# A chain of attention and two MoE blocks: seven instead of eight value products per group in the last two and a half batches of MoE2, over one token buffer

## The chip, the cores and the metric

The kernel runs on one core of one Trainium2 chip. The metric is device time in microseconds: the median of three runs of the whole program.

## The reference, cut to what matters

Attention with a bias from relative positions gives `x` (4 batches x 576 tokens, 512 features). MoE1 takes the maximum of three products and multiplies by `w_out`. MoE2, where the change is made, is

```python
gate = 1.0 / (1.0 + np.exp(-(x @ w_gate)))      # x: 2304 x 512, w_gate: 512 x 1536
val = x @ w_val                                 # w_val: 512 x 1536
return (gate * val @ w_out).astype(np.float32)  # w_out: 1536 x 512
```

All products must be exact to float32. The kernel writes each operand as the sum of two float16 halves, a high one and a low one, and adds three products of halves (high x high, high x low, low x high).

## The kernel before, in words

Every instruction is recorded first (class `Recorder`) and then put in order by a list scheduler (`emit`, `choose`): each engine takes from four classes, `BIAS`, `ATT`, `MOE`, `PREP` in falling priority, the instruction that can start first by the planner's own costs. After that the order on each engine is fixed, and an instruction that waits holds up those behind it on its engine.

MoE2 goes over 4 batches (`b`) of 576 tokens and, in each, over 6 groups of weight columns (`i`). One such step is `quad(b, i)`: 256 gate columns and 256 value columns for 576 tokens, as 2 x 2 blocks of 128 columns by 288 tokens over a depth of 2 x 256.

- The gate blocks are made by Strassen's scheme (Winograd's form): 7 products of block sums instead of 8. Each product is a `group` of 6 matmuls (2 depth steps x 3 products of halves) with 288 moving columns into one PSUM bank. VectorE adds the 7 results up in `sg` (L1279 to L1287); ScalarE copies the first (L592).
- The value blocks are made directly: 8 groups of 6 matmuls into two pairs of banks (`two_r`). ScalarE makes the sigmoid (L1298), VectorE multiplies by the value straight from PSUM (L1300), and the product is split into halves (L1306, and L1096 through `add2`).
- So a quad has 90 matmuls on L1269. The gate parts go through two banks (`part_r`), in the order 1, 6, 7, 5, 2, 3, 4.

The moving operands are the block sums of the tokens, `XC`: 8 slots (slot 7 only for the direct value products), each in two halves. `token_sums` loads a batch from `x_d`, makes the sums (`add2`, L1096) and splits each into halves (`halves`: ScalarE L1102, VectorE L1103). There are two buffers `XC_`, used in turn, so a batch's sums are made while the batch before is multiplied: `next_tokens` is called at the start and in the middle of a batch, in class `ATT`.

The stationary operands are `SW[i]`: 7 gate sums and 4 raw value blocks for each `i`, made early in the stage by `pair_weights`, with the decode from float64 words on VectorE (L554 to L556). `out_weights` does the same for `w_out`, into `OW`; its last part must be done before the first product of `outs`.

`outs` multiplies a finished batch by `w_out`: 36 matmuls with 512 columns (L1325), four evacuations on ScalarE (L1333), one store. In batches 1 to 3 one such call stands behind each of the first four quads; five more are at the end of the kernel. For TensorE they are work that can stand in while MoE2's next quad is not ready. Here `BIAS` is the class of all evacuations.

Of the kernel before, what the change touches and what calls it, by code (L numbers as in the profile page):

```python
# [11 lines left out]
F16 = mybir.dt.float16  # L12
# [3 lines left out]
ALU = mybir.AluOpType  # L16
# [97 lines left out]
class Item:  # L114

    __slots__ = ("k", "cls", "alts", "deps", "left", "users", "end", "done", "banks")

    def __init__(self, k, cls):
        self.k, self.cls = k, cls
        self.alts = {}  # L120
        self.deps, self.users = set(), []
        self.left, self.end, self.done = 0, None, False
        self.banks = set()


class Recorder:
# [10 lines left out]
    def __init__(self, nc, untracked):  # L137
        self.nc = nc
        self.untracked = untracked
        self.items, self.first = [], 0  # L140
        self.mem = Mem()
        self.cls = 0
        self.joined = None
        self.t_eng = {e: 0.0 for e in self.WINDOW}
        self.busy = {e: 0.0 for e in self.WINDOW}
        self.t_dma = 0.0
        self.bank = {i: {} for i in range(8)}
        self.lanes = [0.0] * 8
        self.log = []
        self.passed = {e: False for e in self.WINDOW}  # L150
        for attr, eng in self.ENGINES.items():
            setattr(self, attr, Engine(self, getattr(nc, attr), eng))

    def add(self, eng, method, args, kwargs, call):
# [115 lines left out]
    def choose(self, e, lists, force=False):  # L270
# [3 lines left out]
        for c in range(self.NCLS):  # L274
            ks = lists[e][c]
            seen, w = None, 0
            for it in ks:
# [5 lines left out]
                if it.left:  # L283
                    continue
                s = self.start(it, e, self.SPARE[e], self.LATE)
                if len(it.alts) > 1 and not force:
# [167 lines left out]
def tile_kernel(ctx, tc, q, k, v, w1, b1, w2, mw1, mw2, mw3, mwo, gw, vw, ow, xtab, masks, out):  # L454
# [724 lines left out]

    ob_m = X2[:, 3968:4992]  # L1180
# [55 lines left out]

# [15 lines left out]

    part_r, two_r = Ring([bank(i)[:, 0:HS] for i in (5, 6)]), Ring([bank(i, 1024).rearrange("p (a s) -> p a s", a=2)[:, :, 0:HS] for i in (0, 2)])
    RAW = ((0, 1), (7, 2))

    def quad(b, i):

        h0 = 64 * (b % 2)
        ugm = ug[:, b, i:i + 1]
        sg, XC = sg_r(), XC_[b % 2]  # L1260
        c21, c22, c11, c12 = (sg[:, HS * n:HS * (n + 1)] for n in range(4))
# [3 lines left out]
        def group(ps, W, o, x, start, stop):  # L1265
            with nc.join():
                for kk in range(2):
                    for z, (wp, xp) in enumerate(((0, 0), (0, 1), (1, 0))):
                        nc.tensor.matmul(ps, lhsT=W[:, o, wp, kk], rhs=XC[:, x, xp, kk], start=start and kk == z == 0, stop=stop and kk == 1 and z == 2)  # L1269

        vs = []
        for t, n in enumerate((1, 6, 7, 5, 2, 3, 4)):
            ps = part_r()
            group(ps, SW[i][0], WS[n - 1], n - 1, True, True)
            with nc.at(BIAS):
# [12 lines left out]
            if t in (0, 2, 3, 5):  # L1288
                m, hf = ((1, 0), (1, 1), (0, 0), (0, 1))[(0, 2, 3, 5).index(t)]
                if not hf:  # L1290
                    pv = two_r()
                    vs.append((m, pv))
                for kh in range(2):
                    group(pv[:, hf], SW[i][1], 2 * m + kh, RAW[hf][kh], kh == 0, kh == 1)
        with nc.at(BIAS):
            for m, pv in vs:
                at = sg[:, S * m:S * m + S]
                nc.scalar.activation(at, at, AF.Sigmoid, scale=ugm)  # L1298
                at = at.rearrange("p (a s) -> p a s", a=2)
                nc.vector.scalar_tensor_tensor(at, pv, DOWN2, at, op0=ALU.mult, op1=ALU.mult)  # L1300
        g2 = sg.rearrange("p (m s) -> p m s", m=2)
# [39 lines left out]
    for _ in early:  # L1341
        pass
    token_sums(0, Am[:, 18688:19840], Am[:, 19840:20992], Am[:, 20992:21568])
    mems = parts(Am[:, 18688:22784], [1024, 1024, 512, 512, 512, 512]), parts(X2[:, 2816:6912], [1024, 1024, 512, 512, 512, 512])
# [23 lines left out]
    ends = {0: [], 1: [4], 2: [], 3: [4, 5, 6, 7, 8]}  # L1368
    tx = [X2[:, 4992:5568], X2[:, 5568:6144]]

    def next_tokens(b):
        with nc.at(ATT):
            gx = gm_f[(1, 0, 1)[b]]
            token_sums(b + 1, gx[:, 0:1152], gx[:, 3072:4224], tx[b % 2])

    next_tokens(0)
    for b in range(B):
        with nc.at(BIAS):
            batch_scale(b)
            out_scales(b)  # L1380
        for i in range(NP2):
            quad(b, i)
            for ct in after[b].get(i, ()):
                outs((b if b % 2 else b - 1) // 2, ct)
            if i == 3 and 0 < b < B - 1:
                next_tokens(b)
        if b == 1:
# [36 lines left out]
```

## Time and profile before

| | |
|---|---|
| median of 3 runs | 1040.45 us (1037.43 to 1043.86) |
| the profiled execution | 1040.86 us |
| its span, first to last instruction | 1039.1 us |
[...]

MoE2's quads run from 623.97 us to 995.7 us of the span, with outs between them from 715.2 us on; batch 1 begins at 691.8 us. In a profile, PE is TensorE, PEld its weight loads, DVE VectorE, ACT ScalarE. A busy time is a union: instructions that overlap on an engine count once. A duration is that of one instruction, from its start to the end of its write, so that two that follow each other can overlap; the time from one start to the next is shorter.

### The profile page before, as it was taken

How to read it: one execution, taken by the hardware profiler on the slowest of the kernel's cores; microseconds unless marked ns; L12 is line 12 of the kernel's file. 1: busy time of each engine (PE TensorE's matmuls, PEld its weight loads, DVE VectorE, ACT ScalarE, POOL GpSimd, SP SyncE). 2: the span in 40 equal slices, each digit the busy share in tenths (PEclk: the TensorE clock that was granted, in tenths of full speed). 3: DMA queues.
4: the chain of work that ended last, by engine and by line, in shares of the span. 5: the costliest groups of instructions: out<-in, count | busy, mean ns of one | idle time of the engine just before them, and what ended most of it. 6: DMA issues, size and time to landing. Idle time of an engine off the chain costs nothing.

```text
span 1039.1 us, 21298 instructions
## 1 busy us (share of the span) xinstructions
PE 993.7 (96%) x8156; PEld 670.1 (64%) x8156; DVE 722.9 (70%) x1869; ACT 597.6 (58%) x1336; POOL 120.0 (12%) x146
## 2 busy tenths in 40 slices
PE   4898999997999999999999999999999999999998
PEld 2344577664666666677677777876666656766653
DVE  5788998976878789958779989996354335532320
ACT  6898986775787777856765565653233124222221
POOL 1022114342112322112100100000000000000000
PEclk9999999998999999999999999999999999999999
DMA  7896767567999999875686233420010001000001
GB/s 222 252 303 226 271 211 174 164 165 143 213 228 261 234 219 250 206 199 128 146 181 188 82 104 116 138 62 11 11 67 11 11 11 66 2 11 22 11 11 41
DMA packets 172242, 139.49 MB, mean 134 GB/s; under 512 B 111852, under 2 KB 151020, under 8 KB 171628
## 3 DMA queue, kind: packets, MB, share of 16 engines
q1 hardware_dynamic: 169476, 128.39, 47.6%
q10 hardware_dynamic: 2664, 9.74, 3.3%
q8 instruction: 64, 1.05, 0.4%
q14 instruction: 38, 0.31, 0.1%
HBM read 94.25 MB, written 21.23 MB: 111 GB/s over the span
## 4 chain that ended last, share of the span: by engine, by line
PE 77%; DVE 9%; DMA 3%; issue 2%; ACT 2%; POOL 2%; SPq 0%; ACTq 0%; POOLq 0%; DVEq 0%
PE ps L1269 22%; PE ps L945 19%; PE ps L1325 13%; PE ps L890 7%; PE ps L831 5%; PE ps L863 5%; DMA am<-am 2%; PE ps L834 2%; PE ps L669 2%; POOL am L858 1%; DVE am L1103 1%; DVE am L847 1%; DVE wm L975 1%; PE ps L566 1%; PE ps L611 1%
## 5 line engine op out<-in xcount | busy, mean ns | idle before, releaser
L945 PE MATMUL ps<-wm 128*128 128x320 f16 (+2 forms) x2304 | 304.9, 286 | 0.2 <-DVE am L975 0.2
L945 PEld LDWEIGHTS <-wm 128*128 128x128 f16 x2304 | 222.9, 99 | 54.9 <-issue 3.2
L1269 PE MATMUL ps<-am 128*128 128x288 f16 x1800 | 223.9, 286 | 1.3 <-DVE wm L1300 0.7
L1269 PEld LDWEIGHTS <-am 128*128 128x128 f16 x1800 | 176.1, 98 | 48.5 <-issue 1.6
L1325 PE MATMUL ps<-wm 128*128 128x512 f16 x648 | 142.5, 379 | 0.0
L848 ACT ACTIVATE am<-am,small 128x576 f32<-128x576 f32 (+1 forms) x160 | 123.1, 770 | 30.3 <-DVE small L847 19.4
L847 DVE CUSTOM_DVE_ANT_0 am<-ps,am 128x576 f32<-128x576 f32 (+1 forms) x160 | 117.9, 749 | 28.2 <-issue 13.0
L1325 PEld LDWEIGHTS <-wm 128*128 128x128 f16 x648 | 63.3, 98 | 73.5
L858 POOL TENSOR_SCALAR am<-am,small 128x576 f32<-128x576 f32 (+1 forms) x65 | 64.5, 997 | 206.1 <-DVE small L850 135.5
L890 PE MATMUL ps<-am 128*64 128x128 f32 (+4 forms) x980 | 81.0, 313 | 1.1 <-DVE wm L896 0.7
L592 ACT ACTIVATE am<-ps 128x512 f32<-128x512 f32 (+3 forms) x146 | 66.1, 472 | 26.9 <-PE ps L863 23.5
L863 PE MATMUL ps<-ident,am 128*128 128x128 f32 x450 | 72.2, 282 | 7.5 <-POOL am L858 6.1
L863 PEld LDWEIGHTS ps<-ident,am 128*128 128x128 f32 x450 | 51.1, 143 | 26.1 <-POOL am L858 10.4
L1298 ACT ACTIVATE x<-x,ug 128x576 f32<-128x576 f32 x24 | 18.6, 775 | 77.8 <-DVE x L1287 77.7
L831 PE MATMUL ps<-am 64*128 64x512 f16 (+1 forms) x390 | 55.1, 384 | 7.3 <-DMA am<-am 6.8
L1333 ACT ACTIVATE x<-ps,uo 128x128 f32<-128x128 f32 x64 | 18.2, 368 | 75.3 <-PE ps L1325 55.4
L1298 ACT ACTIVATE wm<-wm,ug 128x576 f32<-128x576 f32 x24 | 18.5, 771 | 56.8 <-DVE wm L1287 56.8
L890 PEld LDWEIGHTS ps<-am 128*64 128x64 f32 x680 | 39.5, 137 | 17.8 <-issue 4.9
L872 DVE SCALAR_TENSOR_TENSOR am<-am,small 128x576 f16<-128x576 f32 (+1 forms) x60 | 48.0, 825 | 3.9 <-ACT am L871 3.8
L975 DVE SCALAR_TENSOR_TENSOR wm<-ps,small,wm 128x256 f32<-128x256 f32 (+1 forms) x84 | 43.0, 512 | 8.5 <-PE ps L945 6.8
L1269 PE MATMUL ps<-am,x 128*128 128x288 f16 x360 | 46.0, 286 | 2.5 <-DVE am L1103 1.9
L871 ACT ACTIVATE am<-am,small 128x576 f16<-128x576 f32 (+1 forms) x60 | 43.6, 766 | 5.3 <-ACT am L848 2.7
(180 smaller groups left out, 1382.6 us busy)
## 6 DMA issues: line engine op xcount, KB each, us to landing
am<-bias_d SPq DMA_DIRECT2D x49, 576.0 KB, 4.6
bias_d<-am SPq DMA_DIRECT2D x36, 320.0 KB, 4.4
wm<-in_moe_w_dram SPq DMA_DIRECT2D x12, 768.0 KB, 6.2
am<-bias_d ACTq DMA_DIRECT2D x15, 576.0 KB, 4.9
wm<-in_moe_w_out_dram SPq DMA_DIRECT2D x24, 256.0 KB, 2.9
x<-in_moe_w_val_dram SPq DMA_DIRECT2D x20, 256.0 KB, 4.1
x_d<-wm SPq DMA_DIRECT2D x4, 1152.0 KB, 4.7
am<-in_v_dram SPq DMA_DIRECT2D x16, 256.0 KB, 5.7
```

Of the source, the lines that this page charges most:

```text
L592: nc.scalar.activation(dst, src, AF.Copy, scale=scale)
L831: nc.tensor.matmul(s_main[o][:m], lhsT=q_[h, eq], rhs=k_[h, ek, 0:512], start=(i == 0), stop=(i == 2), tile_position=(64 * o, 0))
L847: nc.vector.tensor_tensor_reduce(e[:m, c], S_[o][:m], bt[:m, c], -1.0, 3.0e38, ALU.add, ALU.min, mx[:m])
L848: nc.scalar.activation(e[:m, c], e[:m, c], AF.Exp, scale=-1.0, bias=mx[:m], accum_out=l[:m, o:o + 1])
L858: nc.gpsimd.tensor_scalar(e[:m, c], e[:m, c], r[:m, o:o + 1], 1.0, op0=ALU.mult, op1=ALU.mult)
L863: nc.tensor.transpose(ps[:, t], e[:, 128 * (t0 + t):128 * (t0 + t) + 128], ident)
L872: nc.vector.scalar_tensor_tensor(ph[:m, 1, c], e[:m, c], f, ph[:m, 0, c], op0=ALU.mult, op1=ALU.subtract)
L890: nc.tensor.matmul(ps[64 * o:64 * o + 64, :N], lhsT=vv[:, o, tv], rhs=pp[:, tb], start=(i == j == 0), stop=(i == len(todo) - 1 and j == 4) ...
L945: nc.tensor.matmul(ps, lhsT=W(wp, kk), rhs=X(xp, kk), start=(first and i == 0), stop=(last and i == 2))
L975: nc.vector.scalar_tensor_tensor(hv, ps, f, hv, op0=ALU.mult, op1=ALU.max)
L1269: nc.tensor.matmul(ps, lhsT=W[:, o, wp, kk], rhs=XC[:, x, xp, kk], start=start and kk == z == 0, stop=stop and kk == 1 and z == 2)
L1325: nc.tensor.matmul(po, lhsT=g[:, gi, kk], rhs=OW[:, wi, kk], start=(kk == 0 and i == 0), stop=(kk == K2 - 1 and i == 2))
```

## The change

From quad (1, 3) on (`M = 3`), the value blocks are made by the same scheme as the gate blocks. Such a quad is called full here: 7 + 7 groups, 84 matmuls. The value parts follow the gate parts with a lag of two (`LAGV`), through a ring of six banks (`part6_r`). They are added up in a buffer `rv` in SBUF, so the multiply by the sigmoid reads SBUF (L1335 in the changed kernel). The value part of the 15 full quads takes 7 additions and one copy that were not there before.

The sums of value weights this needs are made on chip by `value_sums`, from the halves that are there: the halves are added back to float32, four block sums are formed, and split again. Three of the new sums go to `SV`, one in the place of a raw block. It is called for `i` = 3, 4, 5 in batch 0 and 0, 1, 2 in batch 1, in the lowest class.

`SV` takes the memory of the second token buffer, so there is one `XC`. `token_sums` is now called after the last quad of a batch, in class `BIAS`, its loads earlier; the order of its sums follows the order in which the groups use the slots, and slot 7 is written for batches 0 and 1 only. `ob`, the buffer of outs, is single instead of double.

```diff
-SPLIT5 = True
+M = 3
+LAGV = 2
+CONV = PREP
...
-    XC_ = [Am[:, 14080 + 4608 * i:18688 + 4608 * i].bitcast(F16).rearrange("p (o e k s) -> p o e k s", o=8, e=2, k=2) for i in range(2)]
-    ob_r = Ring([ob_m[:, 512 * i:512 * (i + 1)] for i in range(2)])
+    XC = Am[:, 14080:18688].bitcast(F16).rearrange("p (o e k s) -> p o e k s", o=8, e=2, k=2)
+    SV_f = Am[:, 18688:23296]
+    ob_r = Ring([ob_m])
...
+    def value_sums(i, f):
+
+        f, W = f.rearrange("p (o k f) -> p o k f", o=4, k=2), SW[i][1]
+        nc.vector.tensor_tensor(f, W[:, :, 0], W[:, :, 1], op=ALU.add)
+        a21, a22, a11, a12 = (f[:, o] for o in range(4))
+        add2(a22, a21, a22, ALU.add)
+        add2(a21, a11, a21, ALU.subtract)
+        add2(a11, a22, a11, ALU.subtract)
+        add2(a12, a12, a11, ALU.subtract)
+        halves([SV[i][:, :, e] for e in range(2)], f[:, 0:3], 1.0)
+        halves([W[:, 0, e] for e in range(2)], a12, 1.0)
...
+    def token_sums(b, lo, hi, t, u, raw):
...
-        put(0, b11)
-        put(7, b12)
+        if raw:
+            put(7, b12)
         add2(t, b22, b12, ALU.subtract)
         add2(b12, b12, b11, ALU.subtract)
+        add2(u, b22, b12, ALU.subtract)
+        put(0, b11)
+        put(5, u)
+        put(6, t)
         put(4, b12)
         put(1, b21)
-        add2(b11, b22, b12, ALU.subtract)
-        put(5, b11)
+        add2(b11, b21, u, ALU.subtract)
         put(2, b22)
-        put(6, t)
-        add2(b21, b21, b11, ALU.subtract)
-        put(3, b21)
+        put(3, b11)
...
+        if full:
+            for t in range(7 + LAGV):
+                if t < 7:
+                    part(SEQ[t], 0)
+                if t >= LAGV:
+                    part(SEQ[t - LAGV], 1)
+            with nc.at(BIAS):
+                for m in (1, 0):
+                    at = slice(S * m, S * m + S)
+                    nc.scalar.activation(sg[:, at], sg[:, at], AF.Sigmoid, scale=ugm)
+                    nc.vector.scalar_tensor_tensor(sg[:, at], rv[:, at], DOWN2, sg[:, at], op0=ALU.mult, op1=ALU.mult)
...
-    next_tokens(0)
     for b in range(B):
...
+        if b == 0:
+            gx = gm_f[1][:, 0:1152], gm_f[1][:, 3072:4224]
+            token_loads(1, *gx)
         for i in range(NP2):
             quad(b, i)
+            if (b, i >= M) in ((0, True), (1, False)):
+                with nc.at(CONV):
+                    value_sums(i, cf[b])
...
             if i == 3 and 0 < b < B - 1:
-                next_tokens(b)
+                gx = [gm_f[(1, 0, 1)[b]][:, a:a + 1152] for a in (0, 3072)]
+                token_loads(b + 1, *gx)
+        if b < B - 1:
+            with nc.at(BIAS):
+                token_sums(b + 1, *gx, *tx, b == 0 and M > 0)
```

`part` is the body of the old loop over the seven products, now with the destination `sg` or `rv`. Lines move with the change: the products stand on L1305 (before L1269), the adds on L1315 to L1323 (L1279 to L1287), `halves` on L1114 (L1103), `add2` on L1107 (L1096), outs on L1377 (L1325).

Where the order changes, at three places on VectorE, for which TensorE waits. The first is the edge from batch 0 to batch 1. Before, the token sums of batch 1 (`am<-wm,small,am` and `2x288`) stand between the decodes of `out_weights` (L554 to L556):

```order
L1263 TENSOR_SCALAR ug<-gv_su,ub 128x1
L556 SCALAR_TENSOR_TENSOR wm<-wm 128x256
L555 SCALAR_TENSOR_TENSOR wm<-wm 128x256
L1103 SCALAR_TENSOR_TENSOR am<-wm,small,am 128x576
L1096 TENSOR_TENSOR wm<-x_75,wm 128x1024
L1096 TENSOR_TENSOR wm<-x_75,wm 128x2x64
L556 SCALAR_TENSOR_TENSOR wm<-wm 128x256
L554 TENSOR_SCALAR wm<-wm 128x256
L1096 TENSOR_TENSOR wm<-wm 128x2x288
L555 SCALAR_TENSOR_TENSOR wm<-wm 128x256
L1103 SCALAR_TENSOR_TENSOR am<-wm,small,am 128x576
```

In the changed kernel the same sums stand among the last evacuations (L1323, `x_75<-ps,x_75`) and multiplies (L1352) of quad (0, 5):

```order
L1114 SCALAR_TENSOR_TENSOR am<-wm,small,am 128x576
L567 SCALAR_TENSOR_TENSOR wm<-wm 128x256
L1352 SCALAR_TENSOR_TENSOR x_75<-ps,x_75 128x576
L1323 TENSOR_TENSOR x_75<-ps,x_75 128x288
L1114 SCALAR_TENSOR_TENSOR am<-wm,small,am 128x576 x2
L1352 SCALAR_TENSOR_TENSOR x_75<-ps,x_75 128x576
L1107 TENSOR_TENSOR wm<-wm 128x2x288
L1107 TENSOR_TENSOR x_75<-wm 128x576
L1107 TENSOR_TENSOR wm<-x_75,wm 128x1024
L1107 TENSOR_TENSOR wm<-x_75,wm 128x2x64
L1114 SCALAR_TENSOR_TENSOR am<-x_75,small,am 128x576
L1114 SCALAR_TENSOR_TENSOR am<-wm,small,am 128x576
```

The puts no longer alternate with decodes; they follow the quad's own evacuations, and the decodes give way to them.

The second is the same at the edge from batch 2 to batch 3. Before, the puts stand among the evacuations of quad (2, 4) (`wm<-ps,wm`), one quad early:

```order
L1103 SCALAR_TENSOR_TENSOR am<-wm,small,am 128x576 x2
L1096 TENSOR_TENSOR x_75<-wm 128x576
L1096 TENSOR_TENSOR wm<-wm 128x2x288
L1103 SCALAR_TENSOR_TENSOR am<-wm,small,am 128x576
L1279 TENSOR_TENSOR wm<-ps,wm 128x288
L1096 TENSOR_TENSOR wm<-wm 128x2x288
L1281 TENSOR_TENSOR wm<-ps,wm 128x288
```

In the changed kernel they stand at the end of quad (2, 5) (`x_75<-ps,x_75`):

```order
L1114 SCALAR_TENSOR_TENSOR am<-wm,small,am 128x576
L1317 TENSOR_TENSOR x_75<-ps,x_75 128x288
L1323 TENSOR_TENSOR x_75<-ps,x_75 128x288
L1114 SCALAR_TENSOR_TENSOR am<-x_75,small,am 128x576
L1319 TENSOR_TENSOR x_75<-ps,x_75 128x288
L1320 TENSOR_TENSOR x_75<-ps,x_75 128x288
L1323 TENSOR_TENSOR x_75<-ps,x_75 128x288 x2
L1114 SCALAR_TENSOR_TENSOR am<-x_75,small,am 128x576
L1323 TENSOR_TENSOR x_75<-ps,x_75 128x288 x2
L1335 SCALAR_TENSOR_TENSOR x_75<-x_75 128x576 x2
L1114 SCALAR_TENSOR_TENSOR am<-wm,small,am 128x576 x2
```

The first three puts (slots 0, 5, 6) go before the quad's last evacuation, the next two (4, 1) behind its multiplies (L1335).

The third is quad (3, 4), near the end of the stage. Before, its evacuations and multiplies on VectorE are

```order
L1279 TENSOR_TENSOR wm<-ps,wm 128x288
L1281 TENSOR_TENSOR wm<-ps,wm 128x288
L1283 TENSOR_TENSOR wm<-ps,wm 128x288
L1284 TENSOR_TENSOR wm<-ps,wm 128x288
L1287 TENSOR_TENSOR wm<-ps,wm 128x288 x2
L1300 SCALAR_TENSOR_TENSOR wm<-ps,wm 128x576
L1287 TENSOR_TENSOR wm<-ps,wm 128x288
L1300 SCALAR_TENSOR_TENSOR wm<-ps,wm 128x576
```

and in the changed kernel gate parts (`wm<-ps,wm`) and value parts (`x_75<-ps,x_75`) alternate:

```order
L1315 TENSOR_TENSOR wm<-ps,wm 128x288
L1317 TENSOR_TENSOR wm<-ps,wm 128x288
L1319 TENSOR_TENSOR wm<-ps,wm 128x288
L1320 TENSOR_TENSOR wm<-ps,wm 128x288
L1315 TENSOR_TENSOR x_75<-ps,x_75 128x288
L1323 TENSOR_TENSOR wm<-ps,wm 128x288
L1317 TENSOR_TENSOR x_75<-ps,x_75 128x288
L1323 TENSOR_TENSOR wm<-ps,wm 128x288
L1319 TENSOR_TENSOR x_75<-ps,x_75 128x288
L1320 TENSOR_TENSOR x_75<-ps,x_75 128x288
L1323 TENSOR_TENSOR wm<-ps,wm 128x288
L1323 TENSOR_TENSOR x_75<-ps,x_75 128x288 x2
```

Seven adds from PSUM became fourteen; the two multiplies follow them.

## Rows read from the trace of the kernel before

**Rows 1.** The page: busy time by engine, and busy tenths in 40 slices.
```profile
PE 993.7 (96%) x8156; PEld 670.1 (64%) x8156; DVE 722.9 (70%) x1869; ACT 597.6 (58%) x1336; POOL 120.0 (12%) x146
...
PE   4898999997999999999999999999999999999998
...
DVE  5788998976878789958779989996354335532320
```
**Rows 2.** The page: the chain that ended last, by line, shares of the span.
```profile
PE ps L1269 22%; PE ps L945 19%; PE ps L1325 13%; PE ps L890 7%; PE ps L831 5%; PE ps L863 5%; DMA am<-am 2%; PE ps L834 2%; PE ps L669 2%; POOL am L858 1%; DVE am L1103 1%; DVE am L847 1%; DVE wm L975 1%; PE ps L566 1%; PE ps L611 1%
```
**Rows 3.** Windows: stretch, its length, then busy us by engine, granted clock, DMA.
```profile
640.00:691.00 51.00, 51.00 (x421) 40.78 (x419) 48.90 (x131) 31.46 (x72) 0.00 (x0) 1.00 0.29 91
691.00:707.00 16.00, 12.92 (x101) 9.49 (x99) 15.80 (x38) 7.92 (x20) 0.00 (x0) 1.00 0.17 51
707.00:996.00 289.00, 289.00 (x2005) 195.77 (x2004) 126.95 (x254) 81.13 (x160) 0.00 (x0) 1.00 0.06 21
```
**Rows 4.** The chain in order of time: start us, us, what.
```profile
733.83 11.03 PE ps L1269 x90
744.86 7.77 PE ps L1325 x36
...
995.70 31.79 PE ps L1325 x148
```
**Rows 5.** Waits of TensorE from 690 us on: us in total, times, longest.
```profile
PE ps L1269 <- DVE am L1103: 1.9, 1, 1.9
PE ps L1269 <- DVE wm L1287: 0.5, 1, 0.5
PE ps L1269 <- DVE wm L1281: 0.3, 1, 0.3
PE ps L1269 <- DVE x L1300: 0.3, 1, 0.3
```
**Rows 6.** Timeline of VectorE: start us, us, line, operation, shape, count.
```profile
676.01 0.45 DVE L1283 TENSOR_TENSOR wm<-ps,wm 128x288 f32<-128x288 f32 x1
676.38 0.44 DVE L1284 TENSOR_TENSOR wm<-ps,wm 128x288 f32<-128x288 f32 x1
...
679.05 1.54 DVE L1103 SCALAR_TENSOR_TENSOR am<-wm,small,am 128x576 f16<-128x576 f32 x2
680.51 0.75 DVE L1300 SCALAR_TENSOR_TENSOR wm<-ps,wm 128x576 f32<-128x576 f32 x1
681.18 0.44 DVE L1287 TENSOR_TENSOR wm<-ps,wm 128x288 f32<-128x288 f32 x1
...
684.46 1.41 DVE L1096 TENSOR_TENSOR wm<-wm 128x1024 f16<-128x1024 f32 x2
685.80 0.45 DVE L1281 TENSOR_TENSOR x<-ps,x 128x288 f32<-128x288 f32 x1
...
702.69 0.75 DVE L1096 TENSOR_TENSOR wm<-wm 128x576 f32<-128x576 f32 x1
703.36 0.45 DVE L1281 TENSOR_TENSOR wm<-ps,wm 128x288 f32<-128x288 f32 x1
```
**Rows 7.** Instructions of VectorE by line and shape, 560 to 640 us: busy, mean ns.
```profile
L1103 DVE SCALAR_TENSOR_TENSOR am<-am,gv_su 128x1024 f16<-128x1024 f32 x4 | 5.1, 1276 | 0.0
L1096 DVE TENSOR_TENSOR am<-am 128x256 f32<-128x256 f32 x12 | 4.6, 411 | 0.0
...
L1103 DVE SCALAR_TENSOR_TENSOR am<-am,gv_su 128x512 f16<-128x512 f32 x3 | 2.2, 749 | 0.1
...
L1096 DVE TENSOR_TENSOR wm<-wm 128x1024 f16<-128x1024 f32 x1 | 1.2, 1224 | 0.4 <-ACT wm L1306 0.4
```
**Rows 8.** DMA issues: KB each, median us to landing.
```profile
out_dram<-x SPq DMA_DIRECT2D x16, 256.0 KB, 2.4
...
wm<-x_d SPq DMA_DIRECT2D x6, 576.0 KB, 4.7
```
**Rows 9.** Windows, columns as in rows 3: the last 3 us.
```profile
1036.00:1039.00 3.00, 0.00 (x0) 0.00 (x0) 0.00 (x0) 0.00 (x0) 0.00 (x0) 0.78 0.23 87
```

More of the change, by code (lines that the diff above doesn't have):

```diff
@@ L114 @@
 class Item:
-    __slots__ = ("k", "cls", "alts", "deps", "left", "users", "end", "done", "banks")
+    __slots__ = ("k", "cls", "alts", "deps", "left", "users", "end", "done", "banks", "spare")
     def __init__(self, k, cls):
@@ L123, in __init__ @@
         self.banks = set()
+        self.spare = 0.0
 class Recorder:
@@ L202, in at, with later @@
         self.cls = before
+    @contextmanager
+    def later(self, spare):
+        before, self.spare = self.spare, spare
+        yield
+        self.spare = before
     @staticmethod
@@ L284, in choose @@
                     continue
-                s = self.start(it, e, self.SPARE[e], self.LATE)
+                s = self.start(it, e, self.SPARE[e] + it.spare, self.LATE)
                 if len(it.alts) > 1 and not force:
@@ L1251, in out_scales, with weights @@
         nc.vector.tensor_copy(uox[h0:h0 + 64, b // 2], uo[h0:h0 + 64, b])
-    part_r, two_r = Ring([bank(i)[:, 0:HS] for i in (5, 6)]), Ring([bank(i, 1024).rearrange("p (a s) -> p a s", a=2)[:, :, 0:HS] for i in (0, 2)])
+    bk = [bank(i)[:, 0:HS] for i in range(7)]
+    part_r, part6_r = Ring([bk[i] for i in (5, 6)]), Ring([bk[i] for i in (0, 1, 2, 3, 5, 6)])
+    two_r = Ring([bank(i, 1024).rearrange("p (a s) -> p a s", a=2)[:, :, 0:HS] for i in (0, 2)])
     RAW = ((0, 1), (7, 2))
+    SEQ = (1, 6, 7, 5, 2, 3, 4)
+    def weights(i, j, n):
+        if j == 0:
+            return SW[i][0][:, WS[n - 1]]
+        return SW[i][1][:, {1: 2, 2: 3, 3: 0, 4: 1}[n]] if n < 5 else SV[i][:, {5: 1, 6: 2, 7: 0}[n]]
     def quad(b, i):
@@ L1259, in quad, with group @@
         ugm = ug[:, b, i:i + 1]
-        sg, XC = sg_r(), XC_[b % 2]
-        c21, c22, c11, c12 = (sg[:, HS * n:HS * (n + 1)] for n in range(4))
+        sg, full = sg_r(), (b, i) >= (1, M)
         with nc.at(BIAS):
             nc.vector.tensor_scalar(ugm, scl["gw"][:, 1, i:i + 1], ub[:, b:b + 1], None, op0=ALU.mult)
-        def group(ps, W, o, x, start, stop):
+        def group(ps, W, x, start, stop):
             with nc.join():
@@ L1268, in group, with part @@
                     for z, (wp, xp) in enumerate(((0, 0), (0, 1), (1, 0))):
[L1269 to L1274, printed above, removed]
+                        nc.tensor.matmul(ps, lhsT=W[:, wp, kk], rhs=XC[:, x, xp, kk], start=start and kk == z == 0, stop=stop and kk == 1 and z == 2)
+        def part(n, j):
+            c21, c22, c11, c12 = ((sg, rv)[j][:, HS * q:HS * (q + 1)] for q in range(4))
+            ps = (part6_r if full else part_r)()
+            group(ps, weights(i, j, n), n - 1, True, True)
             with nc.at(BIAS):
@@ L1287, in quad @@
                     nc.vector.tensor_tensor(c, ps, c, op=ALU.add)
[L1288 to L1300, printed above, removed]
+        if full:
[9 more added lines that the diff above has]
+                    nc.vector.scalar_tensor_tensor(sg[:, at], rv[:, at], DOWN2, sg[:, at], op0=ALU.mult, op1=ALU.mult)
+        else:
+            vs = []
+            for t, n in enumerate(SEQ):
+                part(n, 0)
+                if t in (0, 2, 3, 5):
+                    m, hf = ((1, 0), (1, 1), (0, 0), (0, 1))[(0, 2, 3, 5).index(t)]
+                    if not hf:
+                        pv = two_r()
+                        vs.append((m, pv))
+                    for kh in range(2):
+                        group(pv[:, hf], SW[i][1][:, 2 * m + kh], RAW[hf][kh], kh == 0, kh == 1)
+            with nc.at(BIAS):
+                for m, pv in vs:
+                    at = sg[:, S * m:S * m + S]
+                    nc.scalar.activation(at, at, AF.Sigmoid, scale=ugm)
+                    at = at.rearrange("p (a s) -> p a s", a=2)
+                    nc.vector.scalar_tensor_tensor(at, pv, DOWN2, at, op0=ALU.mult, op1=ALU.mult)
         g2 = sg.rearrange("p (m s) -> p m s", m=2)
```

26 lines of the change are left out of this document (14 added, 12 removed).

## The prediction

> **What bounds the kernel now.** I read the page first. TensorE is busy 96% of the span and VectorE 70%; both have a row of slices, and there VectorE is at eight and nine tenths up to the two thirds of the span, then falls to three, while TensorE stays at nine [rows 1]. The chain that ended last is 77% TensorE, and its first line is L1269, the products of MoE2 that the change touches [rows 2]. So the question is whether the stage in which they run waits for anything else. The windows answer it: from 707 us to 996 us TensorE is busy 289.00 of 289.00 us and VectorE 126.95; in the 16 us before, from 691, TensorE is busy 12.92 and VectorE 15.80, and in the 51 us before that 51.00 and 48.90 [rows 3]. The whole stage is thus bound by the number of matmuls, except one place of 16 us where VectorE is full. In the chain a group (quad) of L1269 is 90 matmuls in 11.03 us, a product of outs 36 in 7.77 us, and nothing stands between them [rows 4]. The waits of TensorE from 690 us on are four, all for VectorE, together 1.9 + 0.5 + 0.3 + 0.3 = 3.05 us by the places at 691 to 707 us, which is where batch 1 begins and its token sums come late (L1103) [rows 5].
>
> **What is removed.** A quad has 7 gate products and 8 value products of 6 matmuls. A full quad has 7 and 7. 15 of the 24 quads become full (three in batch 1, six each in batches 2 and 3), so 15 x 6 = 90 matmuls of 288 columns go. One costs 11.03 / 90 = 122.6 ns [rows 4], and the clock is granted in full there [rows 3]. They go from stretches where TensorE is the bound: 90 x 0.1226 = **-11.03 us**. What must hold for it: VectorE, which now also adds up the values, and the new waits must stay hidden.
>
> **VectorE in a full quad.** Its durations overlap: an evacuation of 288 columns lasts 0.45 us, but the next one starts 0.37 us after it, a 576-column L1103 takes 0.73 from start to start, L1300 0.67, the pair of L1096 1.34 [rows 6]. I take the start-to-start times, since an engine that is the bound goes by them. A full quad then has 14 adds x 0.37 + 2 x 0.67 + 1.34 = 7.9 us on VectorE beside 84 x 0.1226 = 10.3 us on TensorE, 2.6 us more than before (7 adds; the multiply is there already). That fits even in the last two quads, which have no outs between them, and six banks in part6_r instead of two let TensorE run ahead by six groups of 0.735 us. ScalarE gets one more copy per full quad. I cost this at nothing. With the 0.45 us in place of 0.37 the quad is 9.0 us, still below 10.3.
>
> **Value sums.** The trace has no value_sums; the nearest rows price it. The add of 1024 elements 1.22 us, four adds of 256 at 0.41, the low halves of 768 between 0.75 (512) and 1.28 (1024), so 1.0, and I take 0.4 for the last 256 [rows 7]: less the 0.08 of overlap for each of the seven, about 3.7 us on VectorE, six times, 22 us. With 15 x 2.6 = 39 us that makes 61 us more in a stretch with 289 - 127 = 162 us free. It is of the lowest class, so it goes where nothing else can start. But three of the six can fall into batch 0, where VectorE has little to spare. What matters there is the order, next.
>
> **The stretch up to the first outs.** I added VectorE's rows in both orders at these prices, from an instruction that both share to the one for which a given product waits. From the 30th to the 330th of L1269's products the changed order has 1.6 to 3.3 us more VectorE work ahead (the value sums of quad 3, one more temporary in token_sums); at the 510th 0.2 more; from the 600th to the 750th 0.7 to 2.2 us less, because the sums of batch 1 no longer stand between the decodes but at the batch's edge. VectorE has 51 - 48.9 = 2.1 us idle in the first of these stretches, so up to 1.2 us of the 3.3 becomes waiting of TensorE; in the second, up to 2.2 of the 3.05 us go. I take 2.05 us of waits for the 3.05 before: **-1.0 us**. Bounds: -3.05 if all these waits go, +3.3 if nothing is given back.
>
> **The handoff.** With one XC the puts of the next batch wait for the last products that read their slot. In batches 2 and 3 that is spread over the last quad, in the order of use: the first three puts stand among its evacuations. At 1 to 2 the tail outs stand in front of the next quad, and 30 of their 36 matmuls wait for nothing: 30 x 7.77 / 36 = 6.5 us of cover [rows 4]. Behind the last product VectorE has one add, two L1300, two puts and the pair of L1096: 0.37 + 1.34 + 1.46 + 1.34 = 4.5 us, and a backlog that I walk to 1.7 us: 6.2, just hidden; 0.2 us. At 2 to 3 there are no such outs; the first put that is late is slot 4, needed by the fifth group, 5 x 0.735 = 3.7 us on, and VectorE needs 0.37 + 1.34 + 0.73 plus 1.2 of backlog: 3.6; 0.4 us. Queued behind a put that waits are the evacuations of the next quad, and TensorE waits for those. Sum **+0.6 us**; bounds 0 and the full chain, in the rivals. At 0 to 1 it is in the stretch above. The token loads take 4.7 us and are issued 5 us ahead of their first reader; ob has one buffer, but a store lands after 2.4 us and the next product of outs ends 7.77 us later [rows 4, 8]: nothing. The end of the kernel, 148 matmuls of outs and the last store, stays as it is [rows 4].
>
> **Sum.** The profiled execution took 1040.86 us for a span of 1039.1. 1040.86 - 11.03 - 1.0 + 0.6 = 1029.4. It lay 0.4 above the median of the three runs, 1040.45, so against that I forecast **1029.0 us**, 1.1% less. A measurement of this kernel tells about 1%, 10.4 us, from no change, so the forecast lies near that edge.
>
> **Rivals.** (a) VectorE becomes the bound in batch 0 and the first half of batch 1. For it: 15.80 of 16 us busy and TensorE's only waits [rows 3, 5]; 2.5 of the value sums (9 us) come in before the first outs, and outs, TensorE's filler, now come 180 products later, behind three full or raw quads more. Against it: the orders' sums above. It loses 6 us instead of winning 1: 1040.45 - 11.03 + 6 = 1035 us.
> (b) The handoff is exposed, and the kernel is slower. One mechanism: single XC, TensorE has nothing to do while the sums are made. Eight puts and four adds, 8 x 0.73 + 4 x 0.67 = 8.5 us at batch 1, seven puts and four adds, 7.8, at batches 2 and 3: 24.1 us, so 1040.45 - 11.03 + 24.1 = 1053 us. It decides from 3.7 us per handoff on (slower at all), and from 7.1 us on it is slower by 1%. For it: the 1.9 us that TensorE waits for exactly such a put today, with two buffers [rows 5]. Against it: the order, which puts three of seven puts before the last product, and the outs.
> On (b) the clock bears. [...] The forecast's waits, under 2 us each, fall in the range in which this trace shows no drop.
> (c) All waits go: 1040.45 - 11.03 - 3.05 = 1026.4.
>
> **How the numbers follow.** The forecast with its own spread of 1026 to 1032 has 0.72, of which 0.52 lie beyond 1% and 0.20 within; (a) 0.18, within; (b) 0.06, slower; (c) or better 0.04, faster. So faster 0.56, same 0.38, slower 0.06. The range: three runs before spread over 6.4 us, so 1 us below (c), 1025.4, and up to (a), 1035.5; what is left out is (b) and little else.
>
> **What would show it.** L1305 with 2070 products, 0.122 us apart; a full quad 10.3 us in the chain; TensorE's waits from 690 us on 2 to 4 us in all; VectorE at some two thirds from the first outs to the last quad; the first outs near 737 us instead of 715. Wrong if TensorE waits more than 1 us at the start of batch 2 or 3, if full quads take over 10.5 us, or if the stretch to the first outs shows waits of over 5 us. The removed matmuls themselves would be wrong only if TensorE had another bound, which 289 of 289 us excludes.

## The result, and the profile after

The changed kernel takes 1025.42 us (median of five runs, 1023.26 to 1033.24) against 1040.45; the ratio is 0.9865, 95% interval 0.9831 to 0.9899. That is 15.0 us less by the medians (10.5 to 17.6 by the interval), where I forecast 11.4. It is inside the forecast range by 0.02 us only (1025.42, lower bound 1025.4), and below the 1026 to 1032 to which I gave most of the chance.

The profiled execution of the changed kernel is the one of 1033.24 us. It reached the first product of MoE2 at 630.62 us, the kernel before at 623.97, and two kernels of this study that are alike up to there reached it at 630.62 and 620.59 (changed, and experiment 5). What the change does is therefore read from that product to the end of the last matmul of outs. I call this the stage: 410.58 us before, 396.28 after, **14.30 us less**. The other 0.7 us of the 15.0 lie outside it, and the part ahead scatters by more than that. In experiments 5 and 6, which cost the stage nothing, it came out the same to 0.01 us.

The page after, busy times and slices, answering [rows 1]:

```profile
PE 987.3 (96%) x8066; PEld 664.4 (64%) x8066; DVE 783.4 (76%) x2015; ACT 610.9 (59%) x1361; POOL 117.9 (11%) x145
...
PE   5898999998999999999999999999999999999998
...
DVE  6788999975778888976678998999967554964530
```

90 matmuls fewer, and VectorE's full stretch is longer. The windows after, columns as in [rows 3]:

```profile
679.00:695.00 16.00, 16.00 (x133) 12.79 (x131) 15.90 (x40) 9.09 (x21) 0.00 (x0) 1.00 0.27 83
695.00:711.00 16.00, 15.66 (x129) 12.39 (x128) 15.78 (x36) 8.75 (x16) 0.00 (x0) 1.00 0.06 18
711.00:727.00 16.00, 16.00 (x132) 12.71 (x130) 15.82 (x37) 9.15 (x21) 0.00 (x0) 1.00 0.16 50
727.00:741.00 14.00, 14.00 (x116) 11.12 (x114) 13.84 (x43) 9.12 (x20) 0.00 (x0) 1.00 0.01 2
741.00:800.00 59.00, 59.00 (x355) 34.63 (x354) 45.15 (x93) 22.72 (x46) 0.00 (x0) 1.00 0.11 39
800.00:890.00 90.00, 90.00 (x619) 60.34 (x617) 51.41 (x112) 25.99 (x55) 0.00 (x0) 1.00 0.08 29
890.00:988.00 98.00, 98.00 (x692) 67.53 (x691) 62.13 (x132) 30.88 (x60) 0.00 (x0) 1.00 0.03 12
```

Up to the first outs (740.62 us) VectorE is busy 61.34 of 62 us and TensorE waits 0.34. After that TensorE is busy all the time, VectorE 64%. TensorE's waits in the whole stage, in the columns of [rows 5]:

```profile
PE ps L1305 <- DVE wm L1352: 0.7, 1, 0.7
PE ps L1305 <- DVE wm L1320: 0.3, 1, 0.3
```

Before there were 3.76 us, the four of [rows 5] and one of 0.7, 14 us after the first product; now there are 1.00. A wait costs the stage 0.16 us more than its row says. The row counts idle time from the end of the matmul before, which comes 0.286 us after its start, while in a row of matmuls the next one starts 0.123 us after it. The durations (ns, least/median/most) of a product:

```profile
L1305 PE MATMUL ps<-am x1758: 282/286/286, 642.1 to 987.8; 128*128 128x288 f16 x196
```

So 90 products (11.03 us), 2.77 us of waits and three waits fewer (0.49 us) make 14.29 of the 14.30 us. The chain in order of time, at the edge from batch 2 to batch 3 and at the end, as [rows 4]:

```profile
874.66 26.46 PE ps L1305 x216
901.12 1.29 PE ps L1377 x6
902.41 0.73 PE ps L1305 x6
903.15 0.65 PE ps L1377 x3
903.79 3.67 PE ps L1305 x30
907.47 5.83 PE ps L1377 x27
913.30 10.29 PE ps L1305 x84
923.59 7.77 PE ps L1377 x36
...
988.06 38.86 PE ps L1377 x180
```

A full quad takes 10.29 us. At the edge (216 products from 874.66 are two quads of batch 2 and eight groups of batch 3) 36 matmuls of outs lie between the first quad's groups, in pieces of 6, 3 and 27.

### The profile page after: what moved, and what is told of

It is laid out like the page before. It is cut to its first block, busy times and chain, and to the rows that moved or that the text cites. A ratio compares the mean times of both kernels' runs of the same rounds, so it can differ in the third digit from the quotient of the medians.

```text
span 1031.5 us, 21363 instructions
## 1 busy us (share of the span) xinstructions
PE 987.3 (96%) x8066; PEld 664.4 (64%) x8066; DVE 783.4 (76%) x2015; ACT 610.9 (59%) x1361; POOL 117.9 (11%) x145
## 4 chain that ended last, share of the span: by engine, by line
PE 56%; DVE 9%; DMA 2%; issue 2%; ACT 1%; POOL 1%; ACTq 0%; SPq 0%; POOLq 0%; DVEq 0%
PE ps L1305 21%; PE ps L1377 14%; PE ps L956 13%; PE ps L901 3%; PE ps L842 2%; DVE am L1114 2%; PE ps L874 1%; DMA am<-am 1%; DVE wm L986 1%; PE ps L845 1%; DVE am L883 1%; DVE am L1107 1%; DMA am<-in_v_dram 1%; POOL am L869 0%; DVE x L566 0%
## 5 line engine op out<-in xcount | busy, mean ns | idle before, releaser
L1305 PE MATMUL ps<-am 128*128 128x288 f16 x1758 | 219.5, 286 | 0.7 <-DVE wm L1352 0.7
L1305 PEld LDWEIGHTS <-am 128*128 128x128 f16 x1758 | 172.0, 98 | 46.8 <-issue 1.1
L1377 PE MATMUL ps<-wm 128*128 128x512 f16 x648 | 142.5, 379 | 0.0
L1377 PEld LDWEIGHTS <-wm 128*128 128x128 f16 x648 | 63.4, 98 | 73.5
L1385 ACT ACTIVATE x<-ps,uo 128x128 f32<-128x128 f32 x64 | 18.2, 368 | 76.0 <-PE ps L1377 38.2
L1323 DVE TENSOR_TENSOR x<-ps,x 128x288 f32<-128x288 f32 x81 | 36.2, 453 | 9.2 <-PE ps L1305 8.9
L782 POOL TENSOR_SCALAR am<-am,small 128x320 f16<-128x320 f32 x48 | 30.7, 656 | 94.1 <-DVE small L777 67.3
L1305 PE MATMUL ps<-am,x 128*128 128x288 f16 x312 | 40.4, 286 | 0.3 <-DVE wm L1320 0.3
```

The lines of the kernel that those rows point to most:

```text
L1305: nc.tensor.matmul(ps, lhsT=W[:, wp, kk], rhs=XC[:, x, xp, kk], start=start and kk == z == 0, stop=stop and kk == 1 and z == 2)
L1377: nc.tensor.matmul(po, lhsT=g[:, gi, kk], rhs=OW[:, wi, kk], start=(kk == 0 and i == 0), stop=(kk == K2 - 1 and i == 2))
```

## The experiments

All values are of the stage as defined above. The expectations of the first eight kernels speak of 357.3 us, which ends where the last 180 matmuls of outs begin; with those, 39.0 us, it is 396.3. I use the latter, since some kernels leave fewer than 180 for the end, and two leave more. Each value is read from one trace, the whole time was measured 10 to 12 times for experiments 1 to 4 and 8 and once for the others. The trace of 8 is of an execution of 1056.91 us, against a median of 1048.08, and is not in the table. The planner orders every kernel anew, so an experiment can also move matmuls of outs.

| | stage, us | TensorE waits in it, us |
|---|---|---|
| before / changed | 410.6 / 396.3 | 3.8 / 1.0 |
| 1 late sums only | 407.5 | 0.8 |
| 2 six products more per full quad | 407.3 | 1.0 |
| 3 two banks | 400.4 | 3.9 |
| 4 M = 0 | 416.8 | 19.6 |
| 5 puts four times | 396.3 | 1.0 |
| 6 low halves four times | 396.3 | 1.0 |
| 7 M = 2 | 404.0 | 6.5 |
| 9 outs away | 397.6 | 2.0 |
| 10 outs away, puts four times | 415.8 | 14.9 |
| 11 M = 6 | 398.7 | 0.8 |
| 12 sums on GpSimd, M = 3 | 414.9 | 15.6 |

**1. The late sums alone.**

```diff
-        sg, full = sg_r(), (b, i) >= (1, M)
+        sg, full = sg_r(), False
...
-            if (b, i >= M) in ((0, True), (1, False)):
+            if False:
...
-                token_sums(b + 1, *gx, *tx, b == 0 and M > 0)
+                token_sums(b + 1, *gx, *tx, True)
```

> The changed kernel with every quad raw and no value sums: 90 products per quad as before, but one token buffer and the token sums behind the last quad of a batch. It does the same 2160 products of MoE2 as the kernel before. Measured from the first product of MoE2 to the start of the last 180 matmuls of outs, the kernel before takes 371.6 us and the changed one 357.3. Theory (the gain is 90 matmuls, and the late order of the token sums takes the waits of batch 1 away): the waits of 3.8 us fall to about 1, so 368.8 us, and the whole time is 0.997 of before. Rival 1 (one buffer exposes the handoff, and only the six banks of the full quads hide it): TensorE waits 2 to 8 us at the start of each of batches 1, 2 and 3, 375 to 390 us, 1.003 to 1.02 of before. Rival 2 (the waits went because of the full quads and not because of the order): 371 to 372 us, 1.00.

Measured: 3.1 us less than before in the stage, as the theory had it (2.8); by the whole time the ratio to before is 0.9974 (0.9933 to 1.0015), no difference by itself. TensorE's waits are

```profile
PE ps L1305 <- DVE wm L1315: 0.6, 1, 0.6
PE ps L1305 <- DVE wm L1317: 0.2, 1, 0.2
```

So the token sums' new place and order, with the one buffer, the earlier loads and the single `ob` that come along, take the waits away without any full quad, and the one buffer costs nothing.

**2. The matmuls given back.**

```diff
             group(ps, weights(i, j, n), n - 1, True, True)
+            if full and j == 1 and n == 4:
+                group(ps, weights(i, j, n), n - 1, True, True)
```

> The changed kernel, but in each full quad the group of six products of value part 4 is done twice into the same bank before it is added: 90 matmuls more, nothing more on VectorE, same output. Theory (the stage goes by the number of matmuls): 15 x 6 x 0.1226 = 11.03 us more, 357.3 becomes 368.3 us from the first product to the last 180 matmuls of outs, 0.997 of before and 1.011 of the changed kernel. Rival (part of the gain comes from elsewhere, and TensorE has slack in the full quads): clearly less than 11 us more, 357 to 363.

Measured: 407.31 against 396.28, 11.03 us more; ratio to before 0.9961 (0.9929 to 0.9992). To the last digit the price of [rows 4]. And 407.31 beside the 407.46 of experiment 1 says that, the products aside, full quads and value sums cost nothing on top of the late sums.

**3. Two banks.**

```diff
-            ps = (part6_r if full else part_r)()
+            ps = part_r()
```

> The changed kernel, but the parts of full quads take their banks from the ring of two that the raw quads have, not from the ring of six. Theory (six banks hide the handoff and the end of each quad, where VectorE does two multiplies and two low halves, 2.7 us, before it comes to the next quad's first part): with two banks TensorE can run ahead by 1.5 us only, so it waits up to 1.2 us at most of the 15 full quads and 2 to 4 us at the start of batch 3: 360 to 378 us in place of 357.3, with TensorE's waits now in many small pieces. Rival (outs and the order of the puts hide it alone, and the ring is of no use): 357 to 358 us, no new waits.

Measured: 4.1 us more, at the low end of the theory's range (3 to 21 more); ratio to before 0.9903 (0.9869 to 0.9938). 2.9 us of it are waits, the longest

```profile
PE ps L1305 <- DVE x L1320: 2.0, 1, 2.0
```

The new waits all lie between 727 and 742 us, around the first outs; none is at the start of batch 3, where the theory had 2 to 4 us, and none at the ends of the later quads. In this kernel's timeline outs stand mostly in threes and sixes among the groups and no longer in blocks of 36. So with outs laid anew the six banks are worth 4 us.

**4 and 7. Earlier full quads.**

```diff
-M = 3
+M = 0
```

> The changed kernel with M = 0 in place of 3: all six quads of batch 1 are full, 18 in all, so 18 matmuls fewer, and all six value sums fall into batch 0. Theory (VectorE has nothing to spare there: it is busy 61 of the 62 us before the first outs): the 18 matmuls give 2.2 us, three more value sums of 3.7 us cost up to 11.1 us on VectorE, so the stage is 1 to 9 us longer than 357.3, and the new waits lie before the first outs. Rival (value sums go into gaps, whatever the batch): 355.1 us, 0.998 of the changed kernel.

(and M = 2:)

> The changed kernel with M = 2: one full quad more, 6 matmuls fewer (0.74 us), and one value sum of 3.7 us more in batch 0. Theory (VectorE has 0 to 1 us to spare before the first outs): 3.7 + 2.6 us more on VectorE there become 3 to 6 us of waits, 359 to 363 us in place of 357.3. Rival (the loss with M = 0 began only when TensorE ran out of raw quads altogether): 356.5 us.

Measured: with M = 0 20.5 us more (ratio to before 1.0044, 1.0009 to 1.0079), with M = 2 7.7 us more, in place of 2.2 and 0.7 less. The expected sign, but more than the forecast (1 to 9, and 1.7 to 5.7). M = 0, waits, timeline of TensorE and windows:

```profile
PE ps L577 <- ACT junk L1220: 14.3, 2, 14.1
PE ps L1377 <- ACT wm L1113: 2.4, 1, 2.4
...
720.47 10.17 PE L1377 MATMUL ps<-wm 128*128 128x512 f16 x35 [0.85 <-DVE wm L1114]
...
701.90:716.00 14.10, 0.04 (x1) 0.00 (x0) 13.69 (x39) 8.07 (x22) 0.00 (x0) 0.61 0.25 78
716.00:720.40 4.40, 1.18 (x3) 0.63 (x4) 4.06 (x16) 2.23 (x6) 0.00 (x0) 0.50 0.00 0
720.40:724.00 3.60, 3.53 (x9) 1.32 (x9) 3.50 (x10) 0.89 (x3) 0.00 (x0) 0.50 0.00 0
```

While TensorE waits, VectorE is busy 13.69 of 14.10 us with the decodes of the out weights and with value sums: it is the bound there, though the row names ScalarE, whose square waits for a decode. There is no raw quad of batch 1 for TensorE to do meanwhile. And the clock comes on top: behind the waits, from 716 to 724 us, 0.50 is granted, and 35 matmuls of outs take 10.17 us (a row of 35 in the changed kernel 7.72). With M = 2:

```profile
698.93 0.39 PE L577 MATMUL ps<-small,ones 128*128 128x6 f32 x2 [0.45 <-ACT junk L1220]
700.54 4.77 PE L1305 MATMUL ps<-am,x 128*128 128x288 f16 x24 [1.22 <-DVE wm L1315]
705.14 1.63 PE L1305 MATMUL ps<-am 128*128 128x288 f16 x12
...
702.00:704.00 2.00, 2.00 (x10) 1.30 (x9) 1.59 (x6) 0.49 (x2) 0.00 (x0) 0.50 0.00 0
```

Two waits of 0.45 and 1.22 us, 0.4 us apart, and behind them 24 products take 4.60 us (700.54 to 705.14) where four groups of 0.735 make 2.94: 1.7 us lost to the clock. The 7.7 us are 5.5 more of waits, 0.16 more for each of four further waits and these 1.7, less 0.7 for the six matmuls; 0.7 I can't place.

**5 and 6. More work for VectorE at the edges and in the full quads.**

```diff
-        put = lambda n, f: halves([XC[:, n, e] for e in range(2)], f, s)
+        def put(n, f):
+            for _ in range(4 if b > 1 else 1):
+                halves([XC[:, n, e] for e in range(2)], f, s)
```

> The changed kernel, but in the token sums of batches 2 and 3 each low half of the seven slots is made four times over (high half on ScalarE too), same values: 21 more of 0.73 us, 15.3 us more on VectorE between the last quad of a batch and the first of the next, twice. Theory (the handoff is hidden with a margin: at 1 to 2 TensorE starts the new batch 0.4 us after the last put has ended, with 6 us of groups to go until it needs the last slot; at 2 to 3 matmuls of outs stand between the first groups): about 6 us of each 15.3 are hidden, TensorE waits 7 to 11 us at either place, 371 to 379 us from the first product of MoE2 to the last 180 matmuls of outs in place of 357.3, and after waits of that length the granted clock falls to half for some us. Rival 1 (no margin): 388 us. Rival 2 (it is hidden by far, since outs and six banks cover more): under 362 us.

```diff
-                add2(lo, src, hi, ALU.subtract)
+                for _ in range(4 if full else 1):
+                    add2(lo, src, hi, ALU.subtract)
```

> The changed kernel, but in full quads the two low halves at the quad's end are made four times over, same values: 3 x 1.34 = 4.0 us more on VectorE per full quad, 11.9 us by my prices beside 10.3 us on TensorE, 60 us in all. Theory (start-to-start prices hold; outs of 7.8 us stand behind most quads, and the six banks lend 4.4 us): only the pairs of quads without outs (fifth and sixth of batches 1, 2 and 3) fall behind, by 1.6 us a quad, so 0 to 4 us in all: 357 to 361 us. Rival (VectorE costs 9.0 us or more per full quad because durations don't overlap there, 13 us with the addition): 5 to 12 us more, 362 to 369.

Measured: 396.27 us both, no new wait. My theory of the edge fell: 15.3 us more at either are hidden (its second rival). 60 us more in the full quads are hidden too. But in both kernels the planner laid the outs anew: in experiment 5 those around the edge from batch 2 to batch 3 stand in pieces of 6 to 27 matmuls instead of 36. What is shown is the room that VectorE has with outs laid in as filler, and not the margin of the changed kernel's own order.

**9 and 10. The edge without outs.**

```diff
-    after = {0: {}, 1: {0: [0], 1: [1], 2: [2], 3: [3]}, 2: {0: [5], 1: [6], 2: [7], 3: [8]}, 3: {0: [0], 1: [1], 2: [2], 3: [3]}}
-    ends = {0: [], 1: [4], 2: [], 3: [4, 5, 6, 7, 8]}
+    after = {0: {}, 1: {0: [0], 1: [1], 2: [2], 3: [3]}, 2: {0: [5, 6, 7, 8]}, 3: {}}
+    ends = {0: [], 1: [4], 2: [], 3: [0, 1, 2, 3, 4, 5, 6, 7, 8]}
```

> The changed kernel with the outs moved: products 5 to 8 of the first pair of batches all behind quad (2, 0), the first four of the second pair behind the last quad. So TensorE has no matmuls of outs at the edge from batch 2 to 3 (in the changed kernel 36 stand between the first products of batch 3), 924 products in a row, the same number in all. Measured from the first product of MoE2 to the end of the last matmul of outs, the changed kernel takes 396.3 us. Theory (my sum's term for this edge, which counted on no outs there: the puts are just late for the fifth group, 0.4 us): 396.3 to 398 us, one or two waits under 1 us at the start of batch 3, and no other. Rival (the outs hide most of the handoff): waits of 3 to 6 us there, 399 to 402.

> As the kernel with the outs moved, and with every put of batches 2 and 3 made four times, 15.3 us more on VectorE at each edge. With the outs in place this cost nothing (396.3 us to the last matmul). Theory (it cost nothing because outs were laid between the groups while VectorE made the puts): at 1 to 2, where outs still stand, nothing; at 2 to 3, with six banks and the order of use left, TensorE waits 8 to 12 us, and the granted clock falls behind it: 404 to 412 us. Rival (six banks and the order of the puts hide it without any outs): 396 to 399.

Measured: 9 takes 1.3 us more, as the theory had it, with two new waits at the start of batch 3:

```profile
PE ps L1305 <- DVE wm L1315: 0.8, 1, 0.8
...
PE ps L1305 <- DVE wm L1317: 0.2, 1, 0.2
```

(1.0 us, and 0.16 more for each of the two.) 10 takes 18.2 us more than 9, all of it at that edge; nothing at 1 to 2, where outs stand. Its timeline of TensorE and windows:

```profile
888.72 0.28 PE L1307 MATMUL ps<-am,x 128*128 128x288 f16 x1 [4.01 <-ACT am L1113]
890.29 3.69 PE L1307 MATMUL ps<-am,x 128*128 128x288 f16 x17 [1.29 <-DVE am L1114]
...
890.00:895.00 5.00, 4.42 (x23) 2.78 (x23) 5.00 (x8) 3.80 (x7) 0.00 (x0) 0.70 0.00 0
```

Neither the order of the puts nor the six banks hide 15.3 us; outs do. The stage is 4 us above the theory's upper bound of 412: ScalarE makes the high halves, four times as well, and 7.6 us of TensorE's waits end with those; and the clock fell (0.70 of full from 890 to 895 us).

**11. No value sums in batch 0** (M = 6).

> The changed kernel with M = 6: only batches 2 and 3 are full, 12 quads, 18 matmuls more, no value sum in batch 0. Theory (with M = 3 VectorE's load before the first outs is just still hidden, so taking it away gives nothing back): 18 x 0.1226 = 2.2 us more, 396.3 becomes 398.5 us from the first product to the last matmul, less the 0.3 us of waits left at batch 1's start. Rival (VectorE's load still costs something that the waits don't show): 396 us or less.

Measured: 2.37 us more, 2.21 for the 18 matmuls. So the theory held. Of 0, 2, 3 and 6, M = 3 is the best.

**8 and 12. The value sums on GpSimd**, with M = 0 and M = 3.

```diff
-        nc.vector.tensor_tensor(f, W[:, :, 0], W[:, :, 1], op=ALU.add)
+        nc.gpsimd.tensor_tensor(f, W[:, :, 0], W[:, :, 1], op=ALU.add)
...
+        g = nc.gpsimd.tensor_tensor
...
+        for d, v in (([SV[i][:, :, e] for e in range(2)], f[:, 0:3]), ([W[:, 0, e] for e in range(2)], a12)):
+            nc.scalar.copy(d[0], v)
+            g(d[1], v, d[0], op=ALU.subtract)
```

(the four `add2` become `g` too; the high halves stay on ScalarE)

> The changed kernel with M = 0 (18 full quads, 18 matmuls fewer than with 3), and with all adds and low halves of the value sums on GpSimd, which does nothing in the whole stage, in place of VectorE. Theory (with M = 0 the loss was VectorE's work alone: three value sums, 11.1 us, and three full quads more, 7.8, less three high puts, against 18.8 us of TensorE waits measured): VectorE has 4 us less than in the changed kernel before the first outs, GpSimd some 6 us per sum by its 128x576 operations of 1.0 us, 33 us in 100; the stage takes 355 to 356 us, 0.998 of the changed kernel and 0.984 of before. Rival (GpSimd takes longer, or slows VectorE's accesses, so that the sums are late): waits of 5 to 20 us remain before the first outs, 360 to 375.

> The changed kernel, M = 3, with the adds and low halves of the value sums on GpSimd. Theory (with GpSimd at work, VectorE's instructions between SBUF tiles take up to twice as long, as 1.22 us for the low half of 1024 elements against up to 2.1 us and 0.29 against 0.72 us for an instruction of the decode with M = 0 on GpSimd; so what VectorE hands over it loses again): three sums in batch 0 keep GpSimd busy about 22 us, VectorE gives up 11 us and loses 6 to 12: 396 to 400 us to the last matmul, with waits of TensorE of 0 to 4 us. Rival (the sums were only late with M = 0, contention is small): 396 us and VectorE clearly less busy before the first outs, 90% or less in place of 98%.

Measured: 8 is slower than before, ratio 1.007 (1.0037 to 1.0102); my theory fell. 12 takes 18.7 us more than the changed kernel, so the move to GpSimd costs this by itself, without M = 0, where my theory had 0 to 4 us. (The 2.1 us in it, from the trace of experiment 8, is of a pair of low halves, of 1024 and of 128 elements, that takes 1.41 us in [rows 6].) The timeline of experiment 12, GpSimd and then VectorE:

```profile
666.23 2.13 POOL L1233 TENSOR_TENSOR x<-am 128x1024 f32<-128x1024 f16 x1
...
681.67 2.19 POOL L1233 TENSOR_TENSOR x<-am 128x1024 f32<-128x1024 f16 x1
...
666.41 2.23 DVE L1114 SCALAR_TENSOR_TENSOR wm<-wm,small 128x256 f16<-128x256 f32 x1
...
682.17 1.84 DVE L565 TENSOR_SCALAR wm<-wm 128x256 int32<-128x256 int32 x1
...
681.80 0.44 DVE L1325 TENSOR_TENSOR wm<-ps,wm 128x288 f32<-128x288 f32 x1
```

VectorE's instruction starts behind GpSimd's and ends 0.15 to 0.3 us after it, at 4.6 and 6.5 times its usual length (0.48 and 0.285 us); the add that reads PSUM takes 0.44 as ever. Over 640 to 745 us, the same groups in the changed kernel and in experiment 12:

```profile
L565 DVE TENSOR_SCALAR wm<-wm 128x256 int32<-128x256 int32 x21 | 5.5, 285 | 0.0
L567 DVE SCALAR_TENSOR_TENSOR wm<-wm 128x256 int32<-128x256 int32 x22 | 9.1, 416 | 0.0
```

```profile
L565 DVE TENSOR_SCALAR wm<-wm 128x256 int32<-128x256 int32 x18 | 10.9, 619 | 0.0
L567 DVE SCALAR_TENSOR_TENSOR wm<-wm 128x256 int32<-128x256 int32 x18 | 11.5, 638 | 0.2
```

These two groups alone lose 10 us (18 x 0.334 + 18 x 0.222), about what three value sums had cost VectorE. How the 18.7 us divide was not separated. But sums that come late from the slower engine are not what TensorE waits for directly: of its 15.6 us of waits 11.7 end with VectorE, 3.9 with ScalarE's squares and none with GpSimd.

## Why the prediction was right, and where not

**The 90 matmuls, -11.03 us:** right. Experiment 2 gives 11.03 back.

**VectorE in a full quad, nothing:** right, and with more reserve than the 2.4 us per quad that I saw: 4.0 more (11.9 beside 10.3) still cost nothing in experiment 6, though with outs laid anew (12 of their matmuls stand between the last products).

**Value sums, 3.7 us each, nothing:** right. The rows of VectorE after:

```profile
L1107 DVE TENSOR_TENSOR x<-x 128x256 f32<-128x256 f32 x20 | 8.0, 418 | 0.2
L1233 DVE TENSOR_TENSOR x<-am 128x1024 f32<-128x1024 f16 x4 | 4.9, 1217 | 0.0
L1114 DVE SCALAR_TENSOR_TENSOR am<-x,am 128x768 f16<-128x768 f32 x5 | 4.8, 951 | 0.9 <-ACT am L1113 0.9
L1114 DVE SCALAR_TENSOR_TENSOR am<-x,am 128x256 f16<-128x256 f32 x5 | 2.1, 416 | 0.0
```

1.22 + 4 x 0.42 + 0.95 + 0.42, less 7 x 0.08, is 3.7. But the reserve is one quad: experiment 7 adds one sum and one full quad before the first outs and loses 7.7 us.

**The stretch up to the first outs, -1.0 us:** mis-sized; of the 3.05 us of waits 0.34 are left, -2.7, near my bound of -3.05. The step that failed is "up to 1.2 us of the 3.3 becomes waiting of TensorE; in the second, up to 2.2 of the 3.05 us go". The first did not happen: the late sums alone leave 0.8 us of waits (experiment 1), with value sums and full quads it is 1.0. In the second nearly all went. In the kernel before, VectorE runs 13 decodes of `out_weights` while TensorE needs the puts of batch 1, from the 540th to the 600th product (lines of 691.85 to 701.68 us, columns as in [rows 7]):

```profile
L555 DVE SCALAR_TENSOR_TENSOR wm<-wm 128x256 int32<-128x256 int32 x5 | 2.1, 414 | 0.0
L556 DVE SCALAR_TENSOR_TENSOR wm<-wm 128x256 int32<-128x256 int32 x4 | 1.6, 412 | 0.0
...
L554 DVE TENSOR_SCALAR wm<-wm 128x256 int32<-128x256 int32 x4 | 1.0, 282 | 0.0
```

In the changed kernel the same 60 products (698.58 to 706.07 us) have none beside them, nor have they in experiment 1. So some 4 us of VectorE's work left this place (4.7 by these durations, which overlap a little); what I had added up was, net of what the change adds, 0.7 to 2.2 less from the 600th to the 750th product. The decodes end 99.9 us after the first product instead of 81.8, and that is still in time, because the first outs, which need them, come after 876 products at 110.0 us instead of after 696 at 91.2. I had these 180 products in the prediction, but only as a loss, in rival (a). That they are what makes the delay harmless is read from the rows, not tried.

**The handoff, +0.6 us:** it cost nothing. The step that failed is "At 2 to 3 there are no such outs". 36 matmuls of outs lie there, those that the program issues behind quad (3, 0), laid between its groups by the planner. Taken away, that edge costs 1.3 us, 1.0 of it in the rows of waits (experiment 9), where I had 0.4 for it. So the price was small as I had it for an edge without outs, if a third of what was measured, and this edge isn't one.

**The sum.** By its steps it should have been -11.03 - 2.77 - 0.49 (three waits fewer) + 0: -14.29, and 14.30 was measured. Loads, the single ob and the end cost nothing: the end has 180 matmuls of outs before and after (the 148 in [rows 4] are a part of them), and from the last one to the end of the span it is 4.5 us, before and after.

**The rivals.** The outcome is (c), 1026.4, to which I gave 0.04: both my wrong terms erred to the same side, since both left out what the planner can put off or lay in at an edge. That the total still fell into the range was close to luck, since the bound lay 1 us below (c) and the part ahead scatters by 10 us. (a), VectorE as the bound before the first outs, is the real limit of the change; it decides at M = 2 and M = 0. (b), the exposed handoff, needs an edge without outs and more work in it than there is: with both, TensorE waits 13.9 us there in experiment 10; with the first alone, 1.0 (experiment 9).

**What would show it.** 2070 products, 10.3 us per full quad, VectorE two thirds: as said. First outs 18.8 us later after the first product; I had 22. Waits from 690 us on 0.3, not 2 to 4.

**The clock.** Around the waits of the kernel before, up to 1.90 us each, the granted clock is 1.00 [rows 3, 5], and in the changed kernel it is 1.00 throughout the stage. In experiment 4 it is 0.50 from 716 to 724 us, behind 14.1 us of waiting, and in experiment 10, with the handoff exposed, 0.70 from 890 to 895 us. That waits under 2 us are safe, as I took from one trace, is refuted by experiment 7 (0.50 from 702 to 704 us, behind waits of 0.45 and 1.22); but one of 2.39 us in the same kernel left the clock at 1.00. What the clock would have cost in (b) no run shows.

## What to carry to other kernels

In this kernel trading matmuls for adds was worth the matmuls to the last digit as long as the adds fell where VectorE was idle. Find the one stretch where it is full, and stop one unit before it overflows, because past it a gain of 0.7 us turned into a loss of 7.7. Before charging a wait at a phase edge, look in the order for work that a planner has laid or can lay there: here it hid 15 us more of puts, and without it the edge as it is cost 1.3 us. Where the part ahead of a change scatters by 10 us, time the stage from its first instruction in the traces.

## What the hardware showed that I had not expected

The slow clock came after waits of 0.45 and 1.22 us close together (experiment 7: 0.50 granted, 1.7 us lost), and not after a single one of 1.90 us in the kernel before (1.00) [rows 3, 5] or of 2.39 further on in experiment 7 itself (1.00 from 720 to 735 us). Behind one of 2.00 in experiment 3 the 36 matmuls of outs took 7.77 us from the first start to the start behind them (732.43 to 740.20), as in [rows 4]. What tells them apart is open.

In experiment 12 instructions of VectorE between SBUF tiles took up to 2.23 us when one of GpSimd was running (2.23 in place of 0.48 and 1.84 in place of 0.29 for the two shown, which end 0.28 and 0.15 us behind it), and those that read PSUM took their usual time (0.44 to 0.46 us for 288 columns). Why was not shown. So an idle GpSimd was no free help for a full VectorE: the move cost 18.7 us.
